# Group 0's queries and keys as 768-byte triples, turned head by head, with another order of chain and requests

## The chip, the cores and the metric

The kernel runs on one core of a Trainium2 chip. The metric is the device time of one execution in microseconds, as the median of several runs. Five engines work side by side, each through its own list of instructions in order: TensorE (PE; its weight loads are listed apart as PEld), VectorE (DVE), ScalarE (ACT), GpSimd (POOL) and SyncE (SP). SP, ACT and POOL also issue the DMA transfers; all of these share the core's 16 DMA engines.

## The reference

Two layers, one after the other. The first is causal attention for 4 batches, 8 heads, 768 tokens and a head size of 64. Heads 0, 2 and 6 see every earlier key ("retrieval"); the other five see only the first 4 keys (the sinks) and a window of the last 64.

```
scores = scale * q @ k.T ; masked where not kept
a = exp(scores - max) ; a = a / (sum(a) + 1e-9)
attn = a @ v                                   # (4, 8, 768, 64)
x = attn.transpose(0, 2, 1, 3).reshape(3072, 512)
p = domain_probs / (sum(domain_probs) + 1e-9)  # (3072, 4)
out = sum over e of p[:, e] * (relu(x @ w1[e]) @ w2[e])
```

The second is a mixture of 4 experts, each 512 to 1024 to 512, applied to every token and added up with the token's weights.

## The kernel before, in words

**Groups and overlap.** Attention is cut into 8 groups g of 384 tokens (4 batches by 2 halves). Group 0 runs alone at the start. From then on the experts' matmuls are the main stream, and a plan with costs (`plan`, `att_ns`, `moe_steps` at the end of the function) slips the steps of the later groups between them. Every engine's order is the order in which the program is written (`manual_schedule`), so a moved line of code moves an instruction on its engine.

**Group 0's chain** is written out by hand in `attention` under `if first:` (lines 940 to 961). Its steps are:
- `transposes(hp)` takes head pair hp = heads 2hp and 2hp + 1. PE turns the float32 rows of q and then of k into PSUM (`transposed`, line 619: three turns of 128 tokens by 128 columns, both heads at once). The turned q is copied to `qT` by ACT for pairs 0 and 2 and by DVE for pairs 1 and 3 (L637). The turned k is copied by DVE, for a retrieval head to `kR` (L645), for the others to `kS` (L661) with their sinks (L669).
- `scores(h)`: PE multiplies q by k (L736), adds a mask as one more matmul (L748, with `bC` or `bS`), ACT takes the exponential into `es` (L754).
- `values(h)` and `values_pair(ha, hb)`: PE multiplies by v (L799, L863, L905); the sums are inverted (DVE L824 to L828, or ACT L878 to L881 and L914 to L915) and DVE scales the result into `xT` (L884, L918), the input of the experts.
- `x_transposes(h)` turns the retrieval heads' results into `xT` (PE L845, DVE L849).
- `warm_up` puts matmuls without use in front of some steps (L480).

`xT` has four chunks of 128 rows. Heads 1 and 5 make chunk 1, heads 0 and 4 chunk 0, heads 2 and 6 chunk 2, heads 3 and 7 chunk 3. The experts' first layer (`plain_steps`, L1148) reads the chunks in the order 1, 0, 2, 3.

**Loads of group 0.** q, k and v come as float32 into the room of `hA`, which the experts use later (`rows32`, lines 393 to 403). Each head of q and of k is one request of 384 rows of 256 bytes (`rows_of`: token j * 128 + p goes to partition p). The loop over `ORDER0` (lines 434 to 455) puts k on SP's queue, q of the first four heads on ACT's and the rest on SP's; v of heads 1, 2, 3 and 6 follows on SP, v of heads 0, 5, 4 and 7 is requested by GpSimd (`request_v`, L419 and L421), which then casts v to half precision (`cast_v`, L432).

**Order on GpSimd.** Identity, masks, requests and casts of v, then `landed(q32[... head 6 ...])` (L552): a copy of one element that waits until q of head 6 is there. Behind it stands `load_w1` of expert 0 (L327), then more casts and `load_w2` of expert 0 (L349), then the later weights and group 1's q and k, with such gates between them. Group 1's q and k are loaded as triples (`load_triples`, L230): partition p takes three tokens in a row, 768 bytes, and `transposed` turns them head by head (L622).

**Fills.** `kS` of group 0 is zeroed by DVE (`zero`, L371). The rows of `vS32` that the sinks of v take (`zeros`) are zeroed by ACT (L457). The sinks of v come by a small request of 8 KB on SP (L439) and are spread over the tiles by GpSimd (`put_sinks_of_v`, L412).

Of the kernel before, what the change touches and what calls it, by code (L numbers as in the profile page):

```python
# [11 lines left out]
FP32 = mybir.dt.float32  # L12
# [3 lines left out]
ENG = mybir.EngineType  # L16
# [3 lines left out]
def kernel(  # L20
# [33 lines left out]
    nc = tc.nc  # L54
    P = 128
    B, H, S, D = q.shape
    E, DM, F = moe_w1.shape
    CH = 3 * P
    NCH = S // CH
    N = B * S  # L60
    HP = H // 2
# [11 lines left out]
    NS = int(n_sink)  # L73
    NW = int(window)
    TK = 96
    R0 = P - TK
# [21 lines left out]
    gp = nc.gpsimd  # L98
# [27 lines left out]
    kS = kSf.rearrange("p (c t s x) -> p c t s x", c=NCH, t=TC, s=NSH)  # L126
# [10 lines left out]
    warm = early[:, 1024:1536]  # L137
    bC = early[:, 1536:1792]
    bS = early[:, 1792:2272].rearrange("p (t x) -> p t x", t=3)
    ident32 = early[:, 2272:2528].bitcast(FP32)  # L140
# [27 lines left out]
    def half(u):  # L168
        return slice(u * D, (u + 1) * D)
# [34 lines left out]
    def rows_of(x, b, h, c):  # L204
        return x[b, h, c * CH : (c + 1) * CH, :].rearrange("(j p) d -> p j d", p=P)
# [167 lines left out]
    def zero(eng, t):  # L373
        fill(eng, t.rearrange("p a b x -> p (a b x)"), 0.0)
# [5 lines left out]
    def one_values(eng, c):  # L380

        one_values_r(eng, 0, c)
        x = vS[:, c, :, :, :]
        if c:
            fill(eng, x[0:R0, :, :, :].rearrange("p t s x -> p (t s x)"), ONES)
        fill(eng, x[:, :, 0:2, D:P], ONES)
        fill(eng, x[:, :, 2:5, 0:D], ONES)
# [4 lines left out]

    def rows32(n):
        x = hA[:, n * 6 * H * D : (n + 1) * 6 * H * D].bitcast(FP32)
        return x.rearrange("p (j h d) -> p j h d", j=3, h=H)

    q32, k32 = rows32(0), rows32(1)
    nc.vector.memset(warm.bitcast(FP32), 0.0)
# [3 lines left out]
    zeros = vS32[0:R0, :]  # L402
# [4 lines left out]
    v_s32 = early[0:NS, 0:1024].bitcast(FP32).rearrange("p (h d) -> p h d", h=H)  # L407

    def put_sinks_of_v():
        for n, m, x in ((0, HP, v_s32[:, 1:H:2, :]), (HP, 1, v_s32[:, HP : HP + 1, :])):  # L410
            x = x.rearrange("p n (t d) -> p n t d", t=1)
            gp.tensor_copy(  # L412
                out=vS32[0:NS, n : n + m, :, :], in_=x.to_broadcast([NS, m, TC, D])
            )

    def request_v(eng, heads):
        for h in heads:
            if RETR[h]:
                eng.dma_start(out=vR32[:, RH.index(h), :, :], in_=rows_of(v, 0, h, 0))  # L419
            else:  # L420
                eng.dma_start(  # L421
                    out=vS32[R0:P, STAGE.index(h), :, :], in_=tiles_of(v, 0, h, 0)
                )
# [7 lines left out]
                in_ = vS32[:, STAGE.index(h), :, :]  # L431
            eng.tensor_copy(out=out_, in_=in_)  # L432

    ORDER0 = (0, 1, 4, 5, 2, 3, 6, 7)
    for n, h in enumerate(ORDER0):
        if n == HP + 1:
            request_v(nc.sync, [1])
        if n == 2:
            nc.sync.dma_start(  # L439
                out=v_s32, in_=v[0, :, 0:NS, :].rearrange("h r d -> r h d")  # L440
            )
        nc.sync.dma_start(out=k32[:, :, h, :], in_=rows_of(k, 0, h, 0))
        if n == HP:

            nc.scalar.add_instruction(
                mybir.InstLoadActFuncSet(
                    name=nc.get_next_instruction_name(),
                    engine=ENG.Activation,
                    act_func_set_id=[x.name for x in SETS].index(
                        "natural_log_exp_and_others"  # L450
                    ),
                )
            )
        eng = nc.scalar if n < HP else nc.sync
        eng.dma_start(out=q32[:, :, h, :], in_=rows_of(q, 0, h, 0))
    nothing = warm.bitcast(FP32)[0:R0, 0:1]
    nc.scalar.copy(out=zeros, in_=nothing.to_broadcast(list(zeros.shape)))  # L457
    request_v(nc.sync, (2, 3, 6))
    nc.sync.dma_start(
        out=probs,  # L460
        in_=moe_domain_probs[0 : NPL * P, :].rearrange("(t p) e -> p t e", p=P),
# [5 lines left out]
    nc.vector.memset(eps, 1e-9)  # L467
    nc.vector.memset(ones, ONES)
    make_identity(nc, ident32)
    one_values(nc.vector, 0)  # L470
    zero(nc.vector, kR[0][:, 0, :, :, :])
    zero(nc.vector, kS[:, 0, :, :, :])
    nc.vector.tensor_copy(out=ident16, in_=ident32)


    ps_warm = pO.tile([P, DM], FP32, name="pO", bufs=2)
# [64 lines left out]
    mask_s(bS[:, 0:2, :], 2, 0.0, -60000.0)  # L541
    gp.tensor_copy(out=bS[:, 2, :], in_=bS[:, 1, :])
    cast_v(gp, [0])
    request_v(gp, [4, 7])
    put_sinks_of_v()
    cast_v(gp, (5, 1))
    k16 = moe.tile([P, H, 3, D], FP16, name="k16", tag="pB", bufs=1)
    qt16 = att.tile([P, H, 3, D], FP16, name="q16", bufs=1)
# [1 line left out]
    def landed(x):  # L550

        gp.tensor_copy(out=seen, in_=x)  # L552
# [6 lines left out]
        return w2sb[0:1, e * FTP, 0:1]  # L559


    landed(q32[0:1, 0, 6, 0:1])
    load_w1(0, 0, F)
    cast_v(gp, (4, 2, 3, 6))
    load_w2(0)
# [34 lines left out]
    def attention(b, c):  # L600
# [9 lines left out]
        def transposed(x, hp):  # L610

            if first or hp > 1:
                ps = bank()
            else:
                ps = pV.tile([P, 512], FP32, name="pV", bufs=2)
            for j in range(3):
                o = ps[:, j * P : (j + 1) * P]
                if first:
                    nc.tensor.transpose(o, x[:, j, 2 * hp : 2 * hp + 2, :], ident32)
                    continue  # L620
                for u in range(2):
                    nc.tensor.matmul(  # L622
                        out=o[u * D : (u + 1) * D, :],
                        lhsT=x[:, 2 * hp + u, j, :],
                        rhs=ident16,
                        start=True,
                        stop=True,
                    )
            return ps
# [209 lines left out]
        def x_transposes(h):  # L839
            ct = PLACE[h][0]  # L840
            x = x_pair if ct else x_one
            r = slice(0, P) if ct else half(0)
            ps = pV.tile([P, 512], FP32, name="pV", bufs=2)
            for j in range(3):
                nc.tensor.matmul(  # L845
                    out=ps[r, j * P : (j + 1) * P], lhsT=x[:, j, r], rhs=ident16,
                    start=True, stop=True,
                )
            nc.vector.tensor_copy(out=xT[g][r, ct, :], in_=ps[r, 0:CH])  # L849
# [90 lines left out]
        if first:  # L940
            yield from transposes(0)
            yield from scores(0)
            yield from scores(1)
            yield from transposes(2)
            yield from values(0)
            yield from scores(4)
            yield from scores(5)
            x_transposes(0)
            yield from transposes(1)
            yield from values_pair(1, 5)  # L950
            yield from scores(3)
            yield from transposes(3)
            yield from scores(2)
            yield from values(4)
            yield from both(scores(6), values(2))
            yield from scores(7)
            yield from values(6)
            yield from values_pair(3, 7)
            x_transposes(6)
            tick(LAG)  # L960
            small_things()
        else:
            order = (0, 2, 6, 1, 3, 5, 7, 4) if by_dma else (0, 2, 1, 3, 6, 5, 7, 4)
            more = divmod(g + 1, NCH) if g + 1 < G else None
            if not by_dma:
                sink_rows(b, c)

            def behind_values(h):
                if more and not RETR[h]:
                    load_v(*more, [h])  # L970
            if by_dma:
                keys_to_rows(b, c)
                yield 1500.0
            else:
                yield from transposes(0)
                yield from transposes(1)

            waiting = []
            for n, h in enumerate(order):
                v_steps, done = iter(()), None  # L980
                ahead = sum(len(score_tiles(x)) for x in (*waiting, h))
                if len(waiting) > 1 or (waiting and ahead > 6):
                    done = waiting.pop(0)
                    v_steps = values(done)
                for m, step in enumerate(both(scores(h), v_steps)):
                    yield step
                    if not by_dma and n == 1 and m == 1:
                        yield from transposes(3)
                if done is not None:
                    behind_values(done)  # L990
                waiting.append(h)
                if n < 3 and by_dma:
                    keys_to_windows(b, c, n)
                if n == 1 and by_dma:
                    sink_rows(b, c)
                if n == 3 and more and g > 1:
                    transpose_rows(*more)
                if not by_dma and n == 2:
                    yield from transposes(2)
            if more:  # L1000
                if g == 1:
                    load_probs(pair0)
                    transpose_rows(*more)
            for h in waiting:
                yield from values(h)
                behind_values(h)
# [714 lines left out]
```

## Time and profile before

| what | value |
|---|---|
| median of 3 runs | 375.99 us (375.68 to 376.76) |
| the profiled execution | 376.48 us |
| its span, first to last instruction | 374.8 us |
| granted TensorE clock | 0.999 of full |
| PE L1148, first start (experts begin) | 20.55 us |
| POOL L327, first start (w1 of expert 0 requested) | 11.23 us |
| SP's last request of group 0 (L463) | 11.13 us |
| DVE L645, first start (first key copy) | 6.04 us |
| POOL L542, end (masks done) | 6.70 us |
| ACT L457, a fill of 32x1280 float32 | 1.26 us |
| DVE L371, a fill of 128x1280 float32 | 1.12 us |
| POOL L412, both copies of the sinks of v | 1.42 us |
| POOL L421, the request of v for heads 4 and 7 | 1.35 us |

Starts are microseconds from the first instruction. A row "start, length, engine, line, operation, out<-in, xcount" merges neighbouring instructions of one kind; the bracket behind it is the time for which the engine sat idle before, and what ended it. The list of waits has the total, the number and the longest. Each execution differs a little: terms read from the profiled one belong to its 376.48 us.

### The profile page before, as it was taken

How to read it: one execution, taken by the hardware profiler on the slowest of the kernel's cores; microseconds unless marked ns; L12 is line 12 of the kernel's file. 1: busy time of each engine (PE TensorE's matmuls, PEld its weight loads, DVE VectorE, ACT ScalarE, POOL GpSimd, SP SyncE). 2: the span in 40 equal slices, each digit the busy share in tenths (PEclk: the TensorE clock that was granted, in tenths of full speed). 3: DMA queues.
4: the chain of work that ended last, by engine and by line, in shares of the span. 5: the costliest groups of instructions: out<-in, count | busy, mean ns of one | idle time of the engine just before them, and what ended most of it. 6: DMA issues, size and time to landing. Idle time of an engine off the chain costs nothing.

```text
span 374.8 us, 10310 instructions
## 1 busy us (share of the span) xinstructions
PE 365.4 (98%) x4219; PEld 310.5 (83%) x4219; DVE 277.9 (74%) x583; ACT 226.3 (60%) x471; POOL 113.0 (30%) x162
## 2 busy tenths in 40 slices
PE   7899899999999999999999999999999999999996
PEld 4655466678998988999989899988899998998995
DVE  4765867797787669868657858857768868979881
ACT  5644569547786785775776855784777361451630
POOL 8845573692057039015501650320000000000000
PEclk9999999999999999999999999999999999999999
DMA  9999999999799399988905990951220300300101
GB/s 181 190 208 207 196 172 191 182 205 106 111 104 160 83 98 129 158 109 76 189 3 65 172 153 13 140 121 12 72 68 2 108 10 2 114 3 14 44 3 58
DMA packets 122340, 39.65 MB, mean 106 GB/s; under 512 B 112192, under 2 KB 114820, under 8 KB 122292
## 3 DMA queue, kind: packets, MB, share of 16 engines
q0 software_dynamic: 82816, 19.01, 57.1%
q1 hardware_dynamic: 37876, 19.58, 23.5%
q8 instruction: 33, 0.54, 0.6%
q10 hardware_dynamic: 1600, 0.39, 0.5%
q14 instruction: 15, 0.12, 0.1%
HBM read 44.89 MB, written 6.34 MB: 137 GB/s over the span
## 4 chain that ended last, share of the span: by engine, by line
PE 85%; DMA 8%; POOL 4%; DVE 1%; issue 1%; ACT 0%; POOLq 0%
PE pO L1462 31%; PE pA L1282 22%; PE pO L1311 9%; DMA w1sb<-in_moe_w_dram 5%; PE pA L1148 5%; PE pA L736 5%; PE pO L1169 5%; DMA q<-in_q_dram 3%; PE pV L1311 2%; PE pA L1311 2%; PE pV L863 2%; PE pV L799 2%; DVE xs L1233 1%; POOL vR L304 1%; PE pA L1554 0%
## 5 line engine op out<-in xcount | busy, mean ns | idle before, releaser
L1462 PEld LDWEIGHTS <-hA 128*128 128x128 f16 x1104 | 104.8, 98 | 11.9
L1282 PE MATMUL pA<-xs,w1sb 128*128 128x256 f16 x768 | 97.2, 272 | 0.0
L1282 PEld LDWEIGHTS <-w1sb 128*128 128x128 f16 x768 | 71.8, 98 | 7.3
L1462 PE MATMUL pO<-w2sb,hA 128*128 128x256 f16 x640 | 76.8, 272 | 0.0
L754 ACT ACTIVATE es<-pA 128x384 f16<-128x384 f32 (+2 forms) x122 | 58.9, 511 | 27.5 <-PE pA L736 22.9
L1291 ACT ACTIVATE hA<-pA 128x512 f16<-128x512 f32 x96 | 57.2, 598 | 29.1 <-PE pA L1282 26.8
L306 POOL DMA_DIRECT2D vS<-in_v_dram x30 | 29.6, 988 | 113.2 <-PE pV L863 109.9
L1462 PE MATMUL pO<-tsb,hA 128*128 128x256 f16 x464 | 56.8, 272 | 0.0
L1233 DVE TENSOR_TENSOR xs<-xT,pB 128x1024 f16<-128x1024 f16 (+1 forms) x49 | 47.0, 976 | 2.7 <-DMA xT<-x_pair 2.7
L1067 DVE TENSOR_TENSOR hA<-hA 128x1024 f16<-128x1024 f16 x60 | 39.4, 684 | 0.6 <-PE pO L1462 0.3
L1161 ACT ACTIVATE hA<-pA 128x384 f16<-128x384 f32 (+1 forms) x64 | 22.2, 385 | 20.4 <-PE pA L1148 20.4
L1311 PEld LDWEIGHTS <-w1sb 128*128 128x128 f16 x512 | 31.3, 98 | 1.6 <-issue 0.5
L1148 PE MATMUL pA<-xT,w1sb 128*128 128x384 f16 (+1 forms) x256 | 30.4, 272 | 1.9 <-DMA w1sb<-in_moe_w_dram 1.8
L1169 PE MATMUL pO<-w2sb,hA 128*128 128x512 f16 x128 | 30.6, 379 | 0.0
L1148 PEld LDWEIGHTS <-w1sb 128*128 128x128 f16 x256 | 19.5, 98 | 10.9 <-issue 2.5
L1482 ACT COPY s<-pO 128x256 f32<-128x256 f32 x31 | 11.5, 372 | 27.3 <-PE pO L1462 21.8
L765 DVE TENSOR_TENSOR es<-es,mS 128x384 f16<-128x384 f16 (+1 forms) x40 | 13.8, 344 | 17.9 <-ACT es L754 17.9
L884 DVE TENSOR_TENSOR xT<-pV,rc 64x384 f16<-64x384 f32 x36 | 20.0, 555 | 8.3 <-ACT rc L881 7.7
L1328 DVE CUSTOM_DVE_ANT_0 hA<-pO,s 128x512 f16<-128x512 f32 x26 | 17.7, 688 | 9.9 <-PE pO L1311 8.5
L878 ACT ACTIVATE rc<-pV,eps 64x384 f32<-64x384 f32 x36 | 20.7, 576 | 6.6 <-PE pV L863 6.0
L1321 ACT COPY s<-pO 128x512 f32<-128x512 f32 x39 | 22.7, 587 | 3.2 <-PE pO L1311 3.0
L736 PE MATMUL pA<-qT,kR 128*128 128x128 f16 (+2 forms) x141 | 23.1, 261 | 0.7 <-DVE kR L645 0.7
(175 smaller groups left out, 519.1 us busy)
## 6 DMA issues: line engine op xcount, KB each, us to landing
pB<-p_rows SPq DMA_DIRECT2D x10, 512.0 KB
out_dram<-o SPq DMA_DIRECT2D x19, 256.0 KB
w1sb<-in_moe_w_dram POOLq DMA_DIRECT2D x8, 512.0 KB, 9.2
w2sb<-in_moe_w_dram POOLq DMA_DIRECT2D x4, 1024.0 KB, 12.1
vS<-in_v_dram POOLq DMA_DIRECT2D x30, 112.0 KB, 4.4
k_rows<-in_k_dram POOLq DMA_DIRECT2D x18, 128.0 KB, 5.3
q<-in_q_dram POOLq DMA_DIRECT2D x18, 128.0 KB, 6.2
out_dram<-hA SPq DMA_DIRECT2D x4, 256.0 KB
```

The lines of the kernel that those rows point to most:

```text
L306: gp.dma_start(out=t[:, :, own_v(h)], in_=windows_of(v, b, h, c))
L736: nc.tensor.matmul(out=ps[:, o : o + nq], lhsT=key_tile(b, c, h, t), rhs=qTs[b, c][:, hp, q0 : q0 + nq], start=(n == 0 or not first), stop ...
L754: nc.scalar.activation(out=es[:, 0:cols], in_=ps[:, 0:cols], func=AF.Exp, scale=SC)
L1067: nc.vector.tensor_tensor(out=out, in0=a, in1=b, op=ALU.subtract)
L1148: nc.tensor.matmul(out=pss[ft][:, 0:cols_n], lhsT=w1_tile(e, ct, ft), rhs=x[:, ct, :], start=(n == 0), stop=(n == DMP - 1),)
L1169: nc.tensor.matmul(out=ps_o, lhsT=hs[:, ft, j * P : (j + 1) * P], rhs=w2sb[:, e * FTP + ft, :], start=(ft == 0), stop=(ft == FTP - 1),)
L1233: nc.vector.tensor_tensor(out=o, in0=xin, in1=pb.to_broadcast([P, DMP, n, P]), op=ALU.mult)
L1282: nc.tensor.matmul(out=ps[:, f * PC : (f + 1) * PC], lhsT=w1_tile(e, ct, f0 + f), rhs=xs[:, ct, :], start=(ct == 0), stop=(ct == DMP - 1),)
L1291: nc.scalar.activation(out=blocks[:, b0 : b0 + 2, k0 : k0 + 2, :].rearrange("p t f x -> p f t x"), in_=ps.rearrange("p (f t x) -> p f t x" ...
L1311: nc.tensor.matmul(out=ps[:, f * P : (f + 1) * P], lhsT=w_tile(e, w[:, ct, :], f), rhs=a[:, ct, :], start=(first and f == 0 and ct == 0), ...
L1321: nc.scalar.copy(out=kept[n], in_=ps)
L1462: nc.tensor.matmul(out=ps, lhsT=a[:, k, :], rhs=b(k), start=(first and k == 0), stop=(k == KT - 1), skip_group_check=not first,)
```

## The change

Three things change for group 0.

**Layout.** q and k are now kept pair by pair. The pairs 1, 2 and 3 (heads 2 and 3, 4 and 5, 6 and 7) are loaded as triples: one request for both heads, 128 partitions by 2 heads by 768 bytes. Pair 0 keeps its two requests of 256-byte rows. `transposed` turns a triple pair head by head: six matmuls of 64 columns against `ident32` in place of three turns of 128, into every third column of the PSUM bank, upper and lower half for the two heads. What is copied from the bank is as before.

**Requests and fills.** SP asks for k of pairs 0, 2, 1, 3, q of pair 3, then v of heads 1, 4, 2, 3, 6, 7; ACT for q of pairs 0, 2, 1. GpSimd asks for the sinks of v ahead of its masks and no longer for v of heads 4 and 7; `put_sinks_of_v` is DVE's, behind the cast of the identity. ACT zeroes `kS` and DVE the `zeros`. The gate ahead of w1 waits for q of pair 3.

**Order of the chain.** `transposes(1)` comes ahead of `scores(5)`, `values(0)` behind it, and `x_transposes(0)` behind `transposes(3)`.

```diff
     def rows32(n):
         x = hA[:, n * 6 * H * D : (n + 1) * 6 * H * D].bitcast(FP32)
-        return x.rearrange("p (j h d) -> p j h d", j=3, h=H)
+        return x.rearrange("p (s x) -> p s x", s=HP)
...
     def put_sinks_of_v():
...
-            gp.tensor_copy(
+            nc.vector.tensor_copy(
...
-    ORDER0 = (0, 1, 4, 5, 2, 3, 6, 7)
-    for n, h in enumerate(ORDER0):
-        if n == HP + 1:
-            request_v(nc.sync, [1])
-        if n == 2:
-            nc.sync.dma_start(
-                out=v_s32, in_=v[0, :, 0:NS, :].rearrange("h r d -> r h d")
-            )
-        nc.sync.dma_start(out=k32[:, :, h, :], in_=rows_of(k, 0, h, 0))
...
-        eng = nc.scalar if n < HP else nc.sync
-        eng.dma_start(out=q32[:, :, h, :], in_=rows_of(q, 0, h, 0))
-    nothing = warm.bitcast(FP32)[0:R0, 0:1]
-    nc.scalar.copy(out=zeros, in_=nothing.to_broadcast(list(zeros.shape)))
-    request_v(nc.sync, (2, 3, 6))
+    def request_rows(eng, x, x32, s):
+        y = x[0, 2 * s : 2 * s + 2, 0:CH, :]
+        if s == 0:
+            for h in range(2):
+                z = x32[:, s, :].rearrange("p (j h d) -> p j h d", h=2, d=D)
+                eng.dma_start(out=z[:, :, h, :], in_=rows_of(x, 0, h, 0))
+            return
+        eng.dma_start(
+            out=x32[:, s, :].rearrange("p (h x) -> p h x", h=2),
+            in_=y.rearrange("h (p j) d -> p h (j d)", j=3),
+        )
+
+    for s in (0, 2, 1, 3):
+        request_rows(nc.sync, k, k32, s)
+        request_rows(nc.sync if s == 3 else nc.scalar, q, q32, s)
...
+    nothing = warm.bitcast(FP32)[:, 0:1]
+    x = kS[:, 0, :, :, :].rearrange("p t s x -> p (t s x)").bitcast(FP32)
+    nc.scalar.copy(out=x, in_=nothing.to_broadcast(list(x.shape)))
+    request_v(nc.sync, (1, 4, 2, 3, 6, 7))
...
     make_identity(nc, ident32)
+    gp.dma_start(out=v_s32, in_=v[0, :, 0:NS, :].rearrange("h r d -> r h d"))
     one_values(nc.vector, 0)
     zero(nc.vector, kR[0][:, 0, :, :, :])
-    zero(nc.vector, kS[:, 0, :, :, :])
+    nc.vector.memset(zeros, 0.0)
     nc.vector.tensor_copy(out=ident16, in_=ident32)
+    put_sinks_of_v()
...
     cast_v(gp, [0])
-    request_v(gp, [4, 7])
-    put_sinks_of_v()
     cast_v(gp, (5, 1))
...
-    landed(q32[0:1, 0, 6, 0:1])
+    landed(q32[0:1, 3, 0:1])
...
                 if first:
-                    nc.tensor.transpose(o, x[:, j, 2 * hp : 2 * hp + 2, :], ident32)
+                    y = x[:, hp, :]
+                    if hp == 0:
+                        nc.tensor.transpose(o, y[:, j * P : (j + 1) * P], ident32)
+                        continue
+                    o = ps[:, 0:CH].rearrange("p (x j) -> p j x", j=3)[:, j, :]
+                    for u in range(2):
+                        n = (u * 3 + j) * D
+                        nc.tensor.matmul(
+                            out=o[half(u), :], lhsT=y[:, n : n + D], rhs=ident32,
+                            start=True, stop=True,
+                        )
                     continue
...
             yield from transposes(2)
+            yield from scores(4)
+            yield from transposes(1)
+            yield from scores(5)
             yield from values(0)
-            yield from scores(4)
-            yield from scores(5)
-            x_transposes(0)
-            yield from transposes(1)
             yield from values_pair(1, 5)
             yield from scores(3)
             yield from transposes(3)
+            x_transposes(0)
             yield from scores(2)
```

More of the change, by code (lines that the diff above doesn't have):

```diff
@@ L432, in cast_v @@
             eng.tensor_copy(out=out_, in_=in_)
-    ORDER0 = (0, 1, 4, 5, 2, 3, 6, 7)
-    for n, h in enumerate(ORDER0):
-        if n == HP + 1:
-            request_v(nc.sync, [1])
-        if n == 2:
-            nc.sync.dma_start(
-                out=v_s32, in_=v[0, :, 0:NS, :].rearrange("h r d -> r h d")
-            )
-        nc.sync.dma_start(out=k32[:, :, h, :], in_=rows_of(k, 0, h, 0))
[L443 to L453, printed above, removed]
-        eng = nc.scalar if n < HP else nc.sync
-        eng.dma_start(out=q32[:, :, h, :], in_=rows_of(q, 0, h, 0))
-    nothing = warm.bitcast(FP32)[0:R0, 0:1]
-    nc.scalar.copy(out=zeros, in_=nothing.to_broadcast(list(zeros.shape)))
-    request_v(nc.sync, (2, 3, 6))
+    def request_rows(eng, x, x32, s):
[12 more added lines that the diff above has]
+        request_rows(nc.sync if s == 3 else nc.scalar, q, q32, s)
+    nc.scalar.add_instruction(
+        mybir.InstLoadActFuncSet(
+            name=nc.get_next_instruction_name(),
+            engine=ENG.Activation,
+            act_func_set_id=[x.name for x in SETS].index("natural_log_exp_and_others"),
+        )
+    )
+    nothing = warm.bitcast(FP32)[:, 0:1]
+    x = kS[:, 0, :, :, :].rearrange("p t s x -> p (t s x)").bitcast(FP32)
+    nc.scalar.copy(out=x, in_=nothing.to_broadcast(list(x.shape)))
+    request_v(nc.sync, (1, 4, 2, 3, 6, 7))
     nc.sync.dma_start(
@@ L618, in transposed @@
                 if first:
-                    nc.tensor.transpose(o, x[:, j, 2 * hp : 2 * hp + 2, :], ident32)
+                    y = x[:, hp, :]
[8 more added lines that the diff above has]
+                            start=True, stop=True,
+                        )
                     continue
```

## The prediction

> **What bounds it now.** The page first: nearly all of the span is TensorE.
>
> ```profile
> span 374.8 us, 10310 instructions
> PE 365.4 (98%) x4219; PEld 310.5 (83%) x4219; DVE 277.9 (74%) x583; ACT 226.3 (60%) x471; POOL 113.0 (30%) x162
> ```
>
> So a start-up change can win only what PE idles. The list of PE's own waits, over the whole span:
>
> ```profile
> PE pA L1148 <- DMA w1sb<-in_moe_w_dram: 1.8, 2, 1.0
> PE pO L480 <- DVE eps L467: 1.3, 1, 1.3
> PE pA L736 <- DVE kS L669: 1.0, 2, 0.5
> PE pA L736 <- DVE kR L645: 0.7, 2, 0.5
> PE pV L480 <- DVE xT L884: 0.5, 1, 0.5
> PE pO L1311 <- ACT hA L1361: 0.2, 1, 0.2
> ```
>
> After 50 us there is only the 0.2 of L1311, so whatever PE is early or late at 50 us it stays so to the end. Two waits are for expert weights (w1); the others lie inside group 0's attention chain. Where they are, from PE's rows in order of time (start, length, count, idle before):
>
> ```profile
> 5.83 0.33 PE L480 MATMUL pA<-early 128*128 128x128 f16 x3
> 7.83 0.88 PE L619 MATMUL pA<-early,hA 128*128 128x128 f32 x6
> 9.43 0.31 PE L736 MATMUL pA<-qT,kS 128*128 128x160 f16 x2 [0.54 <-DVE kS L669]
> 15.77 0.39 PE L736 MATMUL pA<-qT,kR 128*128 128x128 f16 x2 [0.18 <-DVE kR L645]
> 19.43 0.34 PE L845 MATMUL pV<-ident,x_pair 128*128 128x128 f16 x3
> 20.55 5.61 PE L1148 MATMUL pA<-xT,w1sb 128*128 128x384 f16 x32 [0.78 <-DMA w1sb<-in_moe_w_dram]
> 32.57 0.36 PE L622 MATMUL pV<-ident,q 128*64 128x128 f16 x6
> 32.76 0.33 PE L622 MATMUL pV<-ident,k 128*64 128x128 f16 x6
> 46.92 0.81 PE L1148 MATMUL pA<-xT,w1sb 128*128 128x384 f16 x4 [1.01 <-DMA w1sb<-in_moe_w_dram]
> ```
>
> Group 0 leaves PE at 19.77 (19.43 + 0.34). Its last copy, xT of chunk 2 (DVE L849), ends at 20.37; layer 1 takes the chunks in the order 1, 0, 2, 3, so two products of 0.163 (5.61 less one 0.33 drain, by 32) can run before it. Attention alone would let the experts start at 20.1 without loss. They start at 20.55: w1 of expert 0 costs **0.45**. The second weight wait, 1.01 at 46.92, is w1 of expert 2. Together **1.46 us, 0.39%**, is what earlier weights can bring.
>
> What the weights wait for, from the chain and GpSimd's rows:
>
> ```profile
> 11.11 0.18 POOL L552 CAST seen<-hA 1x1 f16<-1x1 f32 x1 [0.75 <-DMA hA<-in_q_dram]
> 11.23 1.25 POOL L327 DMA_DIRECT2D w1sb<-in_moe_w_dram  x2
> ```
> ```profile
> 11.86 8.55 DMA w1sb<-in_moe_w_dram
> 37.21 9.58 DMA w1sb<-in_moe_w_dram
> ```
>
> GpSimd holds w1 back until q of head 6 has landed (11.09). By the table of windows the DMA engines are busy from 2 us on, at 203 to 253 GB/s up to 13 us, nearly all of it in packets under 512 bytes (the last columns are DMA share and GB/s; at 27 us only expert weights move):
>
> ```profile
> 7.00:8.00 1.00, 0.98 (x12) 0.67 (x9) 0.27 (x2) 0.82 (x3) 1.00 (x3) 1.00 1.28 215
> 27.00:28.00 1.00, 1.00 (x7) 0.45 (x5) 0.00 (x0) 0.00 (x0) 0.00 (x0) 1.00 1.11 211
> ```
>
> **Transfers.** Of eight tensors (q and k of four pairs) six change to 768-byte rows: 1.18 MB. At the 215 GB/s of 7 to 8 us they take 5.5 us. The other bound is the weight stage: 211 GB/s written at 27 to 28 us in half precision, so 422 GB/s read from float32 in 4096-byte rows, or 2.8 us. Per packet and engine that is 19 ns for 256 bytes and 155 for 4096; a straight line through both gives 37 ns for 768 bytes, 330 GB/s, 3.6 us. I take **1.9 saved**, between 0 and 2.7. What stands before the gate falls too: v of heads 2, 3, 4, 6, 7 is asked for behind the last q. The 0.39 MB of pair 0 and v of heads 0, 5, 1 (0.29 MB) at 215 GB/s make 3.2 us, with 3.6 and some 0.5 to land, from 1.95: 9.2. Behind it one cast (0.4, L432): w1 is issued at about 9.4, not 11.23. So expert weights land 1 to 1.9 us earlier.
>
> **Queues.** SP issues 14 requests at 0.53 instead of 19, done at 8.2 instead of 11.6; none waits. ACT's four q requests and its fill (1.26, L457) stay, and the filled keys are needed only at 6.62. On GpSimd the sinks' request (0.91, the first L419 row) is moved ahead of the masks: bS, done at 6.70, is done at about 7.6, and PE wants its last third at 7.72; cover 0.1. GpSimd loses 1.35 (two requests) and 1.42 (L412). **DVE gains a wait**: put_sinks_of_v stands behind the sinks' landing. Queued behind it is the kR cast at 6.04, for which PE's first scores wait. Issued at 1.42, behind the identity, and landing in at most the 4.1 that v of head 0 took from issue (96 KB; the sinks are 8), they are there by 5.5; the copies take 1.15 by the 1280-element memset of 1.12. So 0 to 0.6 late; I take **0.1**, since DVE is idle from 4.06 to 6.04 and 8 KB land sooner than 96.
>
> **Turns.** Pair 0 is unchanged. For pairs 2, 1, 3 each of the six tensors was 3 float32 turns, now 6 float32 matmuls of 64 columns: 18 more. Before, 6 turns took 0.88, a slot of 0.122 each (0.88 less one of 0.273, by 5), 0.37 a tensor. No row shows a float32 matmul that isn't a turn. Nearest rows: group 1 turns with the same halves in fp16 (L622), 6 in 0.19 (32.57 to 32.76): 32 ns, against 55 for a full-width fp16 one (L480 at 5.83: 0.33 less 0.219, by 2), so halves do run side by side. **Lower bound**: as fast as that, 0.19 a tensor. **Upper**: four passes one after the other, 6 x 4 x 55 ns = 1.3. **Taken: 0.75**, four passes of halves side by side (4 x 32 x 6 = 0.77), which is also six of the float32 turns' slots (0.73).
>
> What does a tensor at T = 0.75 do to the chain? Follow PE, before's gaps kept (cast of keys and sinks 0.72 from turned keys to scores; scores about 0.5):
> - Pair 2 begins at 7.83 as before, ends at 7.83 + 1.5 + 0.15 of drain = 9.48 (8.71 before); scores of head 4 at 10.2 (9.43).
> - Pair 1 stands right behind them, 10.7 to 12.2 (11.20 to 12.07): here the new order fills a DVE wait. Scores 5 and values 0 to 12.9, the pair 1, 5 at 13.45 (its exponentials end at 13.4), scores 3 at 14.0 (13.52).
> - Pair 3 14.5 to 16.0 (14.02 to 14.84), x_transposes(0) 0.3, scores 2 and values 4 to 17.15: scores 6 at 17.15 (15.77).
> - From there before needed 4.0 to the end; x_transposes' DVE copy, now here, adds 0.1: **21.25 against 19.77, 1.5 late**.
>
> The same walk gives 0 for T = 0.37 (the order alone wins nothing), 0.7 for 0.55, 2.65 for 0.95, 4.75 for 1.3: 4 us per us of T up to 0.75, then 6, as there is no wait left to fill.
>
> **Sum.** Experts could start at 20.1 + 1.5 = 21.6, weights there by 19.4: **+1.05** against 20.55. At 46.92 the wait of 1.01 is gone, as PE comes 1.05 later and the weights no later: **-1.01**. Sinks +0.1. In all +0.14. The profiled execution took 376.48 (span 374.8 and 1.7 around it), 0.5 above the median of 375.99; so 376.6 for it, **376.1** on the median.
>
> **Rivals.**
> 1. *Slower: halves don't overlap in float32.* Place: the six tensors. Price: T = 1.3 makes group 0 4.75 late; 4.3 at the experts' start, 1.01 back: +3.3, **379.3**. It decides from T = 0.94. For it: the float32 turns already need 0.122 where fp16 needs 0.055, and the strided columns are new. Against: fp16 halves overlap. Chance 0.32.
> 2. *Faster: float32 halves cost no more than the turns did*, T of 0.37 to 0.45. Then both weight waits fall, 0.47 and 1.01: -1.5, **374.5**, with the weights 1.5 earlier. Chance 0.13. If 768-byte rows are no faster than 256 (the change not doing what it says), the weights stay and this case is 375.9; the forecast doesn't move, for it asks only that they be no later.
> 3. *The sinks' copy blocks DVE to the full 0.6*: **376.6**. Chance 0.05.
>
> The Trainium skill speaks for rival 1. Its page "FP8 and Floating Point Precision" (TensorE Precision Notes) says that true FP32 takes four passes through the array, "TensorEngine Tiling (Array Packing)" (Restrictions and Gotchas) that column tiling and the FP32 transpose mode exclude each other, and "PSUM — Partial Sum Buffer" (Specifications) that a non-contiguous pattern slows matmuls significantly. Four passes agree with both my T and rival 1's; a stride that also slowed them would give rival 1's 379.3 or more, and no row of before shows such a write.
>
> **Chances.** Forecast 0.50, from T between 0.45 and 0.94, its own range 374.9 to 377.2. A measurement can tell about 0.3%, 1.1 us: faster 0.13, same 0.55 (forecast and rival 3), slower 0.32. The range goes from T = 0.45 (374.8) to T = 1.3 (379.3).
>
> **What would show it.** The slot of the new float32 matmuls out of hA: 0.125 right, 0.2 rival 1, under 0.075 rival 2. The experts' first L1148 at 21.6; no w1 wait at 47; w1 issued at 9.4; kR's first cast at 6.04. It is wrong if PE waits for a turn's bank or for weights still.

## The result and the profile after

The changed kernel takes **378.16 us** (median of 6 executions, 377.51 to 379.21), the kernel before 375.94 on the same chip (6 executions). The ratio is 1.0060, 95% interval 1.0041 to 1.0078: **slower by 0.6%**, 2.2 us. The forecast was 376.1, range 374.8 to 379.3. The profiled execution took 379.21, its span 377.5 and 1.7 around it.

The page first: TensorE is again nearly all of the span.

```profile
span 377.5 us, 10410 instructions
PE 368.8 (98%) x4273; PEld 313.6 (83%) x4273; DVE 278.5 (74%) x585; ACT 226.5 (60%) x471; POOL 112.2 (30%) x159
```

PE is busy 3.4 us longer than before, 2.7 of it in the span. Next PE's longest own waits up to 55 us (us in total, times, longest):

```profile
PE pO L483 <- DVE eps L468: 1.3, 1, 1.3
PE pA L747 <- DVE kR L656: 1.3, 1, 1.3
PE pA L747 <- DVE kS L680: 0.7, 1, 0.7
PE pV L483 <- DVE xT L860: 0.6, 1, 0.6
PE pA L759 <- POOL early L513: 0.4, 1, 0.4
```

No wait for w1 is left, as forecast. Two waits are new in size or kind: 1.3 for the first cast of kR (0.7 before, in two) and 0.4 for a mask. Where they lie, from PE's rows in order of time (start, length, count, idle before):

```profile
7.40 0.39 PE L747 MATMUL pA<-qT,kR 128*128 128x128 f16 x2 [1.26 <-DVE kR L656]
8.84 0.31 PE L759 MATMUL pA<-early,ident 128*128 128x320 f16 x1 [0.44 <-POOL early L513]
9.51 2.83 PE L627 MATMUL pA<-early,hA 128*64 128x128 f32 x24
13.07 0.31 PE L747 MATMUL pA<-qT,kS 128*128 128x160 f16 x2 [0.74 <-DVE kS L680]
13.66 1.53 PE L627 MATMUL pA<-early,hA 128*64 128x128 f32 x24
17.46 1.53 PE L627 MATMUL pA<-early,hA 128*64 128x128 f32 x24
49.66 0.81 PE L1159 MATMUL pA<-xT,w1sb 128*128 128x384 f16 x4
```

The three rows of L627 are the new turns, pairs 2, 1 and 3: twelve matmuls each, which the trace shows as two records apiece. Two take 1.53 us, just the 1.5 of the forecast. The first takes 2.83 for the same work. And it begins at 9.51, not at 7.83: pair 2 is late before a single one of its turns has run. The table of windows tells why the first row is long (PEclk is the column behind POOL, then DMA share and GB/s):

```profile
8.00:9.00 1.00, 0.54 (x6) 0.30 (x5) 0.03 (x1) 0.81 (x2) 0.87 (x4) 0.99 1.22 217
9.00:10.00 1.00, 1.00 (x10) 0.72 (x10) 0.00 (x0) 0.81 (x2) 0.06 (x1) 0.50 1.30 191
10.00:11.00 1.00, 1.00 (x12) 1.00 (x12) 0.00 (x0) 0.00 (x0) 0.34 (x1) 0.50 1.35 186
11.00:12.00 1.00, 1.00 (x14) 0.93 (x10) 0.00 (x0) 0.48 (x1) 0.41 (x2) 0.50 0.83 117
12.00:13.00 1.00, 0.33 (x4) 0.00 (x0) 0.62 (x2) 0.00 (x0) 1.00 (x3) 0.80 0.13 19
```

From 9 to 12.4 us PE runs at half its clock. The reason for the late start is on the two other engines, GpSimd (POOL) and DVE:

```profile
1.66 0.75 POOL L471 DMA_DIRECT2D early<-in_v_dram  x1 [0.28 <-issue]
2.81 1.53 POOL L494 TENSOR_SCALAR_AFFINE_SELECT early<-early 128x128 f16<-128x128 f16 x2
5.79 0.89 POOL L502 MEMSET early<- 128x320 f16 x1
8.75 0.31 POOL L545 COPY early<-early 128x160 f16<-128x160 f16 x1
12.40 1.25 POOL L327 DMA_DIRECT2D w1sb<-in_moe_w_dram  x2
```
```profile
5.70 1.13 DVE L412 COPY hA<-early 4x1024 f32<-4x1024 f32 x2 [1.76 <-DMA early<-in_v_dram]
6.86 0.48 DVE L656 CAST kR<-pA 64x384 f16<-64x384 f32 x1
```

The sinks are asked for at 1.66 and land 3.9 later; DVE waits, copies until 6.83 and only then casts the keys. GpSimd's masks end at 9.06 (8.75 + 0.31); before it was 6.70. And w1 is issued at 12.40, against 11.23 before and 9.4 in the forecast.

The bill in checkpoints of PE, each from one profiled execution. "Experts" is where the experts' first layer would start without a break: its start behind the last wait, less the two products of 0.163 that run ahead of that wait (before has none ahead of it). e1 and e5 are explained below: all of the change but the move of the sinks, in e5 also without the stride of the turns.

| | pair 2's turns | experts | w1 of expert 2 used | span |
|---|---|---|---|---|
| before | 7.83 | 20.55 | 46.92, after 1.01 idle | 374.8 |
| after | 9.51 | 24.50 | 49.66 | 377.5 |
| e1 | 8.52 | 22.22 | 47.37 | 375.1 |
| e5 | 7.78 | 21.48 | 46.69 | 374.4 |

From pair 2 to the experts it is 12.72 before, 13.70 in e1 and in e5, and 14.99 after: turns and order cost 0.98 (net of the 0.45 that the kernel before waits for w1 there), half the clock 1.29 more. With 1.68 of a late pair 2 that makes 3.95; the weights' wait gives 1.01 back, and 2.74 are left at w1 of expert 2, 0.2 less than that sum.

### The profile page after: what moved, and what is told of

Read it like the earlier page. It is cut to its first block, busy times and chain, and to the rows that moved or that the text cites. A ratio compares the mean times of both kernels' runs of the same rounds, so it can differ in the third digit from the quotient of the medians.

```text
span 377.5 us, 10410 instructions
## 1 busy us (share of the span) xinstructions
PE 368.8 (98%) x4273; PEld 313.6 (83%) x4273; DVE 278.5 (74%) x585; ACT 226.5 (60%) x471; POOL 112.2 (30%) x159
## 4 chain that ended last, share of the span: by engine, by line
PE 92%; DVE 4%; POOL 2%; ACT 1%; issue 1%; POOLq 0%
PE pO L1473 31%; PE pA L1293 22%; PE pO L1322 9%; PE pA L1159 7%; PE pO L1180 7%; PE pA L747 5%; PE pV L1322 2%; PE pA L1322 2%; PE pV L810 2%; PE pV L874 2%; PE pA L627 2%; ACT es L765 1%; DVE xs L1244 1%; PE pA L1565 0%; DVE xT L895 0%
```

## The experiments

**Theory**: the loss is the sinks' move (DVE's wait, late masks) and, behind the idling that it brings, the clock; the turns cost what was forecast. **Rivals**: the strided or four-pass turns are what costs; the new order does. Before each run stands what was on record for it.

**e1, the sinks as before**: request back on SP, copies back on GpSimd, all else as changed.

```diff
-            nc.vector.tensor_copy(
+            gp.tensor_copy(
...
+        if s == 0:
+            nc.sync.dma_start(out=v_s32, in_=v[0, :, 0:NS, :].rearrange("h r d -> r h d"))
-    gp.dma_start(out=v_s32, in_=v[0, :, 0:NS, :].rearrange("h r d -> r h d"))
...
-    put_sinks_of_v()
...
+    put_sinks_of_v()
```

The copies stood behind the identity and stand behind the masks again.

> The changed kernel with the sinks of v as before (request on SP behind k of pair 0, copies on GpSimd). Theory S (the sinks' move made the loss beyond the forecast): the first kR cast starts at 6.0 to 6.1 instead of 6.86, the masks are done by 6.8 instead of 9.1, PE never idles over 0.7 us in group 0, the clock stays at full, pairs take 1.47 each, experts begin without loss at about 21.6, time 375.8 to 376.5, which is the record's sum without the sinks. Rival T (the float32 turns and the new order cost more than the walk said): 377.3 to 378.0, with kR early and the experts still at 23 or later.

376.49 us against 376.18, ratio 1.0006 (0.9989 to 1.0022). PE's waits:

```profile
PE pA L750 <- DVE kS L683: 0.7, 1, 0.7
PE pV L485 <- DVE xT L863: 0.6, 1, 0.6
PE pA L750 <- DVE kR L659: 0.4, 1, 0.4
```

The mask's wait is gone, kR's is 0.4, and the clock is 0.999 or 1.0 in all twelve executions. By the medians, most of the 2.2 us hangs on the sinks. But the profiled execution, 376.84, isn't as early as was expected: kR's first cast starts at 6.63 and not at 6.0 to 6.1, pair 2 at 8.52, the experts at 22.22 and not at 21.6. Here it is q of pair 0 that comes late:

```profile
5.08 1.51 PE L625 MATMUL pA<-early,hA 128*128 128x128 f32 x6 [0.22 <-DMA hA<-in_q_dram]
```

The kernel before starts these turns at 4.79 and they take 1.20. e5's profiled execution, 376.09, has the early start as well (kR's cast at 5.89). What makes q land late in some executions is not shown.

**e2, only the request back on SP; e3, only the copies back on GpSimd.** Each is one half of e1's edit.

> The changed kernel with only the sinks' request put back on SP, the copies still DVE's. If the loss is GpSimd's (masks late by the early request): masks done by 6.8, scores of head 1 wait for nothing on GpSimd, and kR depends on when the sinks land through SP: by 5.0 it is at 6.1 and the time 375.9 to 376.5. If the loss is DVE's wait: kR still at 6.7 or later and 376.7 to 377.3. Rival T: 377.3 or more.

> The changed kernel with only the copies put back on GpSimd, the request still GpSimd's and ahead of the masks. Theory S: kR at 6.0 to 6.1; masks still late, done at 7.6 (the request alone) to 8.6 (if the 1.28 us of the first mask select comes with the request), so scores of head 1 wait 0 to 1 us; time 376.0 to 377.2. If the mask fill at 5.79 was held by DVE's copies (0.89 us instead of 0.39), it is back at 0.39. Rival T: 377.3 or more.

e2: 376.84, ratio 1.0016 (1.0000 to 1.0032), 0.35 above e1. e3: 377.20, 1.0027 (1.0007 to 1.0047), 0.71 above e1. Together 1.06, and the changed kernel's executions at full clock (377.51, 377.60, 377.70) lie 1.1 above e1: the two halves add up, though the intervals overlap and the split is rough. The start of pair 2's turns agrees: 8.54 in e2 and 8.80 in e3 are 0.76 and 1.02 later than e5's 7.78, and the changed kernel's 9.51 is 1.73 later (beside e1's 8.52, late for another reason, e2's share would not show). Their waits differ as they should; e2 first, then e3:

```profile
PE pA L750 <- DVE kR L659: 1.7, 1, 1.7
```
```profile
PE pA L759 <- POOL early L512: 1.0, 1, 1.0
PE pA L747 <- DVE kS L680: 0.7, 1, 0.7
PE pA L747 <- DVE kR L656: 0.5, 1, 0.5
```

In e2 the keys wait for DVE, in e3 the masks for GpSimd. GpSimd's rows split the lateness of the masks: e3 has the long selects without DVE's copies (the third row is DVE's fill of `zeros`),

```profile
2.80 1.54 POOL L493 TENSOR_SCALAR_AFFINE_SELECT early<-early 128x128 f16<-128x128 f16 x2
5.79 0.38 POOL L501 MEMSET early<- 128x320 f16 x1
2.73 1.12 DVE L474 MEMSET hA<- 32x1280 f32 x1 [0.20 <-DVE kR L371]
```

and the kernel before shows both short:

```profile
1.71 0.55 POOL L491 TENSOR_SCALAR_AFFINE_SELECT early<-early 128x128 f16<-128x128 f16 x2
3.93 0.39 POOL L499 MEMSET early<- 128x320 f16 x1
```

So moving the request ahead costs its own 0.75, 0.3 of issue and 1.0 more in the selects behind it, all of it in the first (1.28 instead of 0.29). What holds that select is not shown. It now stands behind a request, but also, 1.1 us later than before, beside DVE's fill of `zeros`, and it ends at 4.09, 0.24 behind that fill's end at 3.85; a fill of DVE's that lay beside the selects of the kernel before (1.99 to 2.53) didn't lengthen them. No run separates the two. The other 0.5 is the memset, 0.89 instead of 0.38, which lies beside DVE's copies (5.70 to 6.83). In e2 it is a smaller memset that lies beside them, and it takes 0.68 instead of 0.25. The Trainium skill's page "SBUF — State Buffer" (Terms) says that DVE and GpSimd share a pair of ports which one of them holds for a whole instruction while the other blocks; both memsets agree with it.

**e4, PE kept busy while it waits**: the changed kernel, with 20 matmuls of zeros ahead of the first scores instead of 3.

```diff
-        WARM = {("s", 0): 3, ("v", 1): 3, ("v", 3): 4, ("v", 2): 2, ("v", 6): 2}
+        WARM = {("s", 0): 20, ("v", 1): 3, ("v", 3): 4, ("v", 2): 2, ("v", 6): 2}
```

> The changed kernel with 20 warm-up matmuls instead of 3 ahead of the first scores, which fill 0.94 us of PE's idle 1.26. Theory C (idling PE lost its full clock, in some executions only): no execution has a granted clock under 0.998, all lie at 377.3 to 377.8, pair 2's turns take 1.5 us and not 2.8. Rival: the low clock has another cause, and some executions still lie at 378.5 to 379.3 with 0.995.

377.63, between 377.50 and 377.95, all 12 executions at a mean clock of 0.999 or 1.0; pair 2's turns take 1.53. Of the changed kernel's six executions three had 0.994 or 0.995, and those are the three above 378.6. Half a clock for 3.4 us is so worth 1.3 us in about half of the executions. That PE's idling sets it off rests on this run, 0 of 12 executions against 3 of 6. How much idling it takes is open: e2's one gap of 1.70 us and e3's gaps, with PE busy for 1.73 and 1.65 of the 3 us from 6 to 9, left the clock at full in all 24 executions, and of the 35 executions of the kernel before that go with e1 to e4 two had 0.995. The Trainium skill's page "TensorE: Matmul & The Clock Gate" (What's actually happening) knows the half clock and puts it behind at least one idle window of about 3.4 us. The half and the 3.4 us agree. But PE was not idle for a window here: it ran for 1.29 of the 3 us from 6 to 9 (0.15, 0.60 and 0.54). The measurement decides: a stretch with gaps is enough, at times.

**e5, the turns without the stride**: e1, but the new matmuls write adjacent PSUM columns. The tokens of pairs 1 to 3 of group 0 stay in the order of the triples, so this part is not the reference's.

```diff
-                    o = ps[:, 0:CH].rearrange("p (x j) -> p j x", j=3)[:, j, :]
```

> As e1 (sinks as before), but the 36 turns of pairs 1 to 3 write adjacent PSUM columns instead of every third; what is changed in the computation: the tokens of these pairs stay in the order of the triples. My theory (the stride costs nothing, a float32 matmul of 64 columns takes about 0.12 us by its four passes): 24 records of one pair stay at 1.46 to 1.53 us, the time at 376.5. Rival (the stride is what makes them slower than fp16 halves, the PSUM rule): the 24 records fall to 1.1 or less, group 0 ends over 1 us earlier.

376.36 against 376.08, ratio 1.0009 (0.9991 to 1.0028). The row of pair 2's turns:

```profile
7.78 1.53 PE L629 MATMUL pA<-early,hA 128*64 128x128 f32 x24
```

1.53, as with the stride: in float32 the stride costs nothing, and the rival falls.

**e7, half by half**: e1 with the same matmuls in another order, three of one head and then three of the other.

```diff
+            for u, j in itertools.product(range(2), range(3)):
+                if first and hp:
+                    o = ps[:, 0:CH].rearrange("p (x j) -> p j x", j=3)[:, j, :]
+                    n = (u * 3 + j) * D
+                    nc.tensor.matmul(
+                        out=o[half(u), :], lhsT=x[:, hp, n : n + D], rhs=ident32,
```

> As e1, the same 36 matmuls in another order: the three of one head, then the three of the other, so that only one of five neighbours writes the other half of the columns. My theory (two neighbours of different halves share the array in float32): with nothing to share with, a pair takes up to 2.5 us instead of 1.47, group 0 comes about 2 to 3 us later, 378 to 379.5. Rival (the halves never overlapped; 0.061 per record is just what a float32 matmul of 64 columns costs): 1.47 per pair stays, 376.5.

376.85 against 376.08, ratio 1.0015 (1.0000 to 1.0029). A pair takes more, but far less than the 2.5 expected, and the time stays below the 378 to 379.5 expected:

```profile
8.21 1.80 PE L639 MATMUL pA<-early,hA 128*64 128x128 f32 x24
```

So halves of the array do overlap, but the price without it is small: a record every 66 ns instead of 55 ((1.80 - 0.27) / 23 and (1.53 - 0.27) / 23). An estimate from both: I count the step between the two records of one matmul, and that between neighbours of the same half, as steps to the same half (12 + 8 of 23 here, 12 in e1), the rest as steps to the other half (3 here, 11 in e1); then a step to the same half is 71 ns and one to the other 37. Then even with no overlap at all a tensor, 12 records, takes 0.85 us, not 1.3.

**e8, the order before**: e1, with the chain as in the kernel before.

> As e1, with the chain in the order of the kernel before (values 0 ahead of scores 4, pair 1 behind scores 5, the transposed input behind scores 5). My walk: with a pair at 1.5 us the new order is worth 0.57 us, because pair 1's turns fill the wait for the cast of pair 2; so the old order gives +0.5, 377.0. Rival (order is worth nothing, as for turns at their old length): 376.5, with the same end of group 0.

376.90 against 376.08, ratio 1.0025 (1.0014 to 1.0035); 0.54 above e5 on the same chip, 0.41 above e1. In the profiled execution it is 14.20 us from pair 2's turns (8.40) to the experts (22.60), against 13.70 in e1 and e5: 0.50. The walk's 0.57 holds: the new order is a gain, once the turns are long.

**e9, cast first**: e1, with the triples of pairs 1 to 3 cast to fp16 on GpSimd, ACT and DVE, and turned in fp16. This takes the float32 turns of these pairs away.

```diff
+    cast_rows(gp.tensor_copy, k16a, k32, 2)
...
+            cast_rows(nc.scalar.copy, q16a, q32, 2)
...
+            cast_rows(nc.vector.tensor_copy, q16a, q32, 1)
+            cast_rows(nc.vector.tensor_copy, k16a, k32, 1)
...
+            cast_rows(nc.scalar.copy, q16a, q32, 3)
+            cast_rows(nc.scalar.copy, k16a, k32, 3)
...
-                            out=o[half(u), :], lhsT=y[:, n : n + D], rhs=ident32,
+                            out=o[half(u), :], lhsT=(k16a if x is k32 else q16a)[:, 2 * hp + u, j, :],
+                            rhs=ident16,
```

> As e1, with the triples of pairs 1 to 3 cast to fp16 before they are turned (pair 2's keys on GpSimd, its queries on ACT, pair 1 on DVE, pair 3 on ACT) and turned by fp16 matmuls; the weights' gate stands ahead of two of GpSimd's casts of values. My theory (the turns' four passes are the 0.3 that e1 has left over the kernel before): a pair falls from 1.47 to about 0.4 us, group 0 ends about 1.5 earlier, the experts start when w1 has landed, 374.5 to 375.5. Rival (the casts come to stand where the turns stood: DVE, ACT and GpSimd late with kR, masks or exponentials): 376.5 or more, with new waits of PE for ACT, POOL or DVE casts of q and k.

375.70 against 376.08, ratio 0.9999 (0.9984 to 1.0013): 0.8 below e1, about half of what was hoped for, and by the interval no faster than the kernel before. Both sides were partly right:

```profile
8.24 0.85 PE L641 MATMUL pA<-ident,tsb 128*64 128x128 f16 x12
10.46 0.31 PE L763 MATMUL pA<-qT,kS 128*128 128x160 f16 x2 [1.37 <-DVE kS L696]
```

The turns shrink to 0.85, not to 0.4, and behind them PE waits 1.37 instead of 0.73: DVE casts pair 1's keys, which landed late, ahead of head 4's. Executions run from 375.1 to 377.6, two of the twelve at a mean clock of 0.995.

**e10, that cast on ACT** behind the copy of pair 2's queries, and the weights' gate on pair 1's keys; **e11**, e10 with five matmuls of zeros ahead of head 4's scores; **e12**, e11 with w2 of expert 2 asked for ahead of two loads of values.

```diff
-            cast_rows(nc.vector.tensor_copy, k16a, k32, 1)
             yield from transposes(2)
+            cast_rows(nc.scalar.copy, k16a, k32, 1)
...
-    landed(q32[0:1, 3, 0:1])
+    landed(k32[0:1, 1, 0:1])
```
```diff
-        WARM = {("s", 0): 3, ("v", 1): 3, ("v", 3): 4, ("v", 2): 2, ("v", 6): 2}
+        WARM = {("s", 0): 3, ("s", 4): 5, ("v", 1): 3, ("v", 3): 4, ("v", 2): 2, ("v", 6): 2}
```
```diff
-    load_v(0, 1, SH[:2])
     load_w2(2)
-    load_v(0, 1, SH[2:])
+    load_v(0, 1, SH)
```

> As e9, with the cast of pair 1's keys on ACT behind the copy of pair 2's queries (in e9 it stood on DVE ahead of head 4's keys and PE idled 1.37 us for them), and the weights' gate on the keys of pair 1 instead of the queries of pair 3. My theory (that cast is what held the scores of head 4; an idle PE of 1.4 us is what let the clock fall in some of e9's executions): PE's wait there falls from 1.37 to about 0.75, the scores of head 4 start at 9.85 instead of 10.46, w1 is issued at 10.1 instead of 10.98, the experts start 0.6 earlier, 374.6 to 375.2, and executions of 376.8 and more become rare. Rival (pair 3's rows and the values then share the DMA engines with the weights and come late, or the weights take as long as before in the end): new waits for pair 3 or for w1 of expert 2, 375.5 to 376.

> As e10, with five matmuls of zeros ahead of the scores of head 4, in PE's remaining wait of about 0.75 us. My theory (it is the idle PE that costs the clock): nothing in the best executions, and no execution at half clock at all, so the spread is below 0.8 us; the median equals e10's, or lies below it by the share of executions that e10 loses. Rival (the clock falls by chance, not by idling): the same share of slower executions as in e10.

> As e11, with w2 of expert 2 asked for ahead of the values of group 1's two first sink heads instead of behind them. My theory (e11's executions of 376.8 and more are those in which w2 of expert 2 lands late, 2.2 us late at 55.3 in its profile, with PE at half clock for some 4 us behind the wait): w2 is asked for 1.3 us earlier, most such executions fall back to 374.6 to 375.0, the median to about 375. Rival (all that moves on the DMA engines between 10 and 55 us is too much for an earlier PE, whatever its order): the late transfer is another, the values of group 1 or w1 of expert 2, and the executions spread as in e11, median 375.3 to 376.

e10: 375.81 against 376.12, ratio 0.9989 (0.9971 to 1.0006). The wait fell to 0.7 and w1 was issued at 9.78, but PE now waits 1.0 for w1 of expert 2, and executions spread from 374.2 to 377.6: the rival's price, at the median. e11: 375.29, ratio 0.9988 (0.9960 to 1.0015), with five of twelve executions above 376.7, so the theory that PE's gap before head 4 makes them was wrong. The profiled execution is the slowest of these, 379.51, and the only one of the twelve at a lower mean clock (0.995):

```profile
PE pO L1201 <- DMA w2sb<-in_moe_w_dram: 2.2, 1, 2.2
```
```profile
54.00:55.00 1.00, 0.00 (x0) 0.00 (x0) 0.04 (x1) 0.00 (x0) 0.00 (x0) 1.00 1.39 178
55.00:56.00 1.00, 0.68 (x3) 0.29 (x3) 0.00 (x0) 0.00 (x0) 0.44 (x1) 0.92 1.41 188
56.00:57.00 1.00, 1.00 (x9) 0.65 (x8) 0.00 (x0) 0.04 (x1) 0.44 (x1) 0.50 1.24 183
```

w2 of expert 2 is 2.2 us late at 55.3, and right behind that wait the clock is 0.50 again. Whether the other four, at full clock, also waited for w2, no run shows. e12: **375.22 against 376.46, ratio 0.9969 (0.9947 to 0.9992)**, the first version that beats both kernels clear of the noise. Two of its twelve executions lie above 376.7, against five in e11, but the median is e11's 375.29 within the noise: that asking for w2 earlier did it is not shown.

**e13, fp16 without the stride**: e12 with e5's edit, and the tokens of pairs 1 to 3 again in the order of the triples.

> As e12, with the fp16 turns of pairs 1 to 3 writing adjacent PSUM columns instead of every third; what is changed in the computation: the tokens of these pairs stay in the order of the triples. In e9 twelve strided fp16 halves took 0.85 us (two every 0.11), while six of group 1's, which write adjacent columns, took 0.19 in the kernel before (two every 0.055). My theory (in fp16 the stride doubles the price of a turn, which the four passes of float32 hide): the twelve take about 0.55 us. Rival (the difference comes from where the operands lie or from the two separate tensors): 0.85 stays.

374.27 against 376.10, ratio 0.9953 (0.9936 to 0.9969), in four executions. e12 and then e13, one pair each:

```profile
7.48 0.85 PE L640 MATMUL pA<-ident,tsb 128*64 128x128 f16 x12
```
```profile
8.24 0.54 PE L639 MATMUL pA<-ident,tsb 128*64 128x128 f16 x12
```

In fp16 the stride does cost: one matmul of these lasts 314 ns with it and 219 without, and the twelve 0.31 more.

## Why the prediction came out as it did, step by step

The time fell inside the range, but on the side that had a chance of 0.32, and not by that side's mechanism. That the range held it is luck: its upper end was there for rival 1, not for the sinks or the clock.

- **The turns: right.** T was taken at 0.75 a tensor and is 0.73: in e1 pair 1's turns begin at 11.38 and the scores behind them at 12.85, 1.47 for two tensors. Of the reason given, e7 bears out the halves side by side; that there are four passes no run shows, for the trace has two records a matmul.
- **The walk: right.** Experts 1.05 late by turns and order was the forecast; e5 shows 0.93 (21.48 against 20.55). e1's profiled execution is 1.67 late, but 0.69 of that is there before pair 2 begins. The order's worth, put at 0.57 for e8, is 0.4 to 0.5 there. The wait of 1.01 is gone.
- **"-1.01" at w1 of expert 2: right, with a remainder.** In e1 a wait of 0.28 for DVE's copy of group 1's queries (L651) stands at 51.3, where the kernel before has none: its wait for weights had covered that work. Of e1's 0.3 above the kernel before 0.04 was forecast. This wait may be part of it, and q of pair 0 landing late another; the interval of e1 doesn't tell the 0.3 from no difference.
- **The sinks, "I take 0.1": the step that failed.** DVE's term was 0 to 0.6 and GpSimd's a cover of 0.1 for masks that were to end at 7.6. Measured in e2 and e3 it is 0.35 and 0.71, in all 1.06. Three things were missing: the request goes out at 1.66 and not at 1.42, and then takes 3.9 for 8 KB, though I had counted on few bytes landing soon; the first select behind it takes 1.0 longer; and a memset beside DVE's copies takes 0.5 longer. The masks ended at 9.06. Rival 3 had the place right, but only at DVE, at half the price and with a chance of 0.05.
- **Full clock throughout: not asked.** That an idle PE could be paid for twice was in no term. It is worth 1.3 us in three of six executions; without it the median would be 377.6.
- **"w1 is issued at about 9.4": wrong, and harmless.** It was 12.40, and with the sinks as before still 11.02 (e1) and 12.04 (e5). "None waits" was said of SP's queue. In e1 it stands still four times, 2.4 us in all, until rows of q have gone; the values of head 1 are asked for at 5.4 there and land at 10.56, and GpSimd, whose casts stand ahead of the gate, is idle for the last 0.93 us of that. The 768-byte rows themselves did move at 311 to 366 GB/s between 5 and 8 us, by the windows (1133 of 1537 packets there had 512 bytes or more), where 330 was the estimate. PE came late enough for all of that not to matter.
- **Rival 1** (halves that don't overlap, or a stride that slows them): wrong in both. Its 379.3 was nearly the profiled execution's time, with another cause. The rule of the Trainium skill's page "PSUM — Partial Sum Buffer" (Specifications), weighed there, holds in e13's fp16 and not in e5's float32. That the passes of float32 leave the PSUM write the time it needs was only argued.

The sum in its place, on the median: 0.3 for turns, order and rows (e1), 1.1 for the sinks (e2 and e3), and 0.6 for the clock (378.16 less the 377.60 of the middle execution at full clock), 2.0 in all; measured 2.2. The rest is within the interval of e1.

## What to carry to other kernels

A small request or copy that is moved "out of the way" is priced by what stands behind it on both queues and by its landing, not by its bytes: here 8 KB cost 1.1 us, while the 36 large matmuls that looked dangerous cost what they were worked out to. Where PE idles in pieces near the start, look whether the next windows still show full clock, for the idle time may be paid again. And when a stage gets shorter, ask for the next transfer in line: in their profiled executions e10 to e12 still wait for expert weights (1.0 for w1 in e10, 2.2 for w2 in e11, 0.4 for w1 in e12).

## What the runs showed of the hardware that was not expected

- The clock falls to 0.50 for 3.4 us, once, behind gaps that PE has worked between (after: 9.0 to 12.4) or one gap of 2.2 (e11: 55.9 to 59.3). e2 has one gap of 1.70 in its profile, and full clock in all twelve executions.
- With the early DMA request ahead of them, two GpSimd selects last 1.0 us longer (1.53 and 1.54, against 0.55); whether the request holds the first of them or DVE's fill beside it, no run here shows.
- A float32 matmul of 64 columns is two records of about 55 ns, with a stride of three columns or without; in fp16 the same stride makes 314 ns of 219.
- 8 KB asked for by GpSimd took 3.9 us to land, nearly as long as 96 KB did before (4.1).
